# In a slot of the attention loop, the second step of a head's output in front of the first transposes of the next head

## The chip, the cores and the metric

The kernel runs on one NeuronCore of a Trainium2 chip. The metric is the device time of one execution in microseconds (us), lower is better. The core has five engines that work side by side, each through its own queue of instructions in a fixed order: TensorE (PE, matmuls; its weight loads are listed apart as PEld), VectorE (DVE), ScalarE (ACT), GpSimd (POOL) and SyncE (SP, which here only starts transfers, DMAs). An instruction starts when all before it in its queue have started and the semaphores that it waits for have been raised by other engines or by DMAs.

## The reference

Eight batches of eight heads of attention (576 positions, 64 dimensions a head) with a mask by blocks of 64, then a feed-forward part with a product of two projections:

```python
scores = scale * np.matmul(q, k.transpose(0, 1, 3, 2))     # q, k, v: (8, 8, 576, 64)
mask = (pos[:, None] // 64) >= (pos[None, :] // 64)
scores = np.where(mask, scores, -1000000000.0)
scores = scores - np.max(scores, axis=-1, keepdims=True)
attn = np.exp(scores)
attn = attn / (np.sum(attn, axis=-1, keepdims=True) + 1e-09)
attn_out = np.matmul(attn, v)
...
x = attn_out.transpose(0, 2, 1, 3).reshape(4608, 512)
out = ((x @ w_a) * (x @ w_b)) @ w_out                      # w_a, w_b: 512x1536, w_out: 1536x512
```

## The kernel before

The program has two parts. The first, up to about 640 us, is a loop over 66 slots (`for s in range(NH + LAG)`): it computes the attention of 64 heads and, between the attention's steps, the first pass of the feed-forward part (a third of the hidden columns) for the tokens that are done, 36 matmuls a slot in the long run. The second part, from there to the end, computes the other two thirds of the hidden columns, with weights that DVE unpacks from 64-bit numbers as it goes.

Three Python generators make a head's attention, and each call of `next` on one writes out a step of it:

- `softmax` (S): the head's scores in four blocks of query rows, each block's maximum (DVE, L398) and exponentials (ACT, L401). The last step sums up and inverts the sums (DVE, `rc`, L435 to L442), and POOL multiplies the five tiles of exponentials `e` by them (L445), first the tile of the last block, `e_3`.
- `turn` (T): four groups of transposes of the scaled `e` tiles by PE (L468, tiles `tp`), from block 3 down to block 0. I call them T3, T2, T1, T0. For each, ACT copies the result to `ah` (L470) and, from the ninth head on, DVE computes the remainder `al` (L472). The remainders of T1 and T0 are put behind the inversion `rc` of the next head in DVE's queue (`behind_of(..., "rc")`).
- `values` (V): the head's output. From the ninth head on its first step, V1, is four matmuls with `ah` (L517), and its second, V2, six matmuls that also read `al` (L521, L523), two copies by ACT (L527, L530) and four additions by DVE (L528 to L532). At every second head V2 also splits the finished x into two parts (ACT and POOL, L110 and L113: `xh`, `xl`) and starts a DMA of x to memory from ACT's queue (L539). For the first eight heads ("native", plain 32-bit matmuls) the output is one run of 16 matmul calls with `ah` alone (L499 to L512), split between the two steps.

A slot `s` runs the steps that the list `SLOT` names: which generator, for which head relative to `s`, and a weight `m` by which feed-forward matmuls are dealt out after the step. So a head's scores come in slot `s`, its T3, T2 and T1 in slot `s+1`, its T0, V1 and V2 in slot `s+2`. The loop counts the steps with a weight in `k`; at certain values of `k` it also writes out the split of the next pair's q and k (`split_q`, `split_k`: ACT L337 and L344, DVE L338, POOL L345) and the copying of these to both halves of the partitions (`spread`, DMAs).

The order in which Python writes the instructions out is not yet the order in the queues. A scheduler takes them by that order as a priority, but lets an engine go on with a later one where, by its own reckoning of time, an earlier one is not ready. A changed `SLOT` therefore moves instructions on all engines.

Buffers that matter here: the `tp` tiles in PSUM have two buffers, which T0 to T3 and the small output tile `av0` of V2 share in turn; the output tile `av` has one.

In front of the loop and in slots 0 and 1 some matmuls on zeros are put in (`WARM`, `KEEP`), whose results nobody reads. The weights of the first pass are unpacked in the first dozen slots by DVE (`convert`, L139 to L149, five instructions for each of twelve tiles), with one ACT instruction (L140) and copies by ACT and POOL.

Of the kernel before, what the change touches and what calls it, by code (L numbers as in the profile page):

```python
# [52 lines left out]
def attention_then_bilinear_ffn(  # L53
# [529 lines left out]
    def want(now):  # L583

        n = (now - H - LAG) * per_slot - behind
        if now < 2 * H + LAG:
# [6 lines left out]
    S_, T_, V_ = softmax, turn, values  # L593

    SLOT = [(S_, 0, 3), (S_, -1, 0), (T_, -2, 4), (S_, 0, 4), (V_, -2, 3), (S_, 0, 3),
            (T_, -1, 4), (V_, -2, 3), (S_, 0, 3), (T_, -1, 5), (T_, -1, 4)]
    fill = sum(m for _, _, m in SLOT)
    gens = {}
    for s in range(NH + LAG):
# [294 lines left out]
```

## Time and profile before

| what | value |
|---|---|
| median of three runs | 1281.07 us (1278.56 to 1282.27) |
| the profiled execution | 1281.83 us, its span 1279.8 us |
| busy share of the span | PE 97%, PEld 92%, DVE 78%, ACT 53%, POOL 43% |
| TensorE clock granted over the span | 0.988 of full speed |
| instructions | 23524, of them 7849 matmuls |

The span goes from the first to the last instruction; 2.0 us of the execution's time lie outside it. A busy share counts the time in which at least one of an engine's instructions is under way. The ends of matmuls are modelled and matmuls overlap, so a busy PE need not run at its peak. The granted clock is told as a share of full speed; 1.00 is 2.4 GHz and 0.50 is 1.2 GHz, and it knows only these two levels here.

### The profile page before, as it was taken

Reading aid. Unit: us, or ns where it says so; the run is one execution under the profiler, and the core shown is the slowest. Engines: PE = TensorE matmul, PEld = TensorE weight load, DVE = VectorE, ACT = ScalarE, POOL = GpSimd, SP = SyncE. Lnnn points to the kernel's source line nnn. Section 1 sums busy time; section 2 is a strip of 40 time slices with the busy share of each in tenths; the row PEclk is TensorE's granted clock in tenths of the full one; section 3 lists DMA queues with packets and bytes.
Section 4 is the critical chain, followed back from the end, with each engine's and each line's share of the span. In section 5 each row is a group of like instructions: output and inputs, shape, how many; then the busy total and the mean of one; then the engine's idle time right before and its main releaser. Section 6 shows DMA issues by size and latency. Waiting matters only on the chain.

```text
span 1279.8 us, 23524 instructions
## 1 busy us (share of the span) xinstructions
PE 1239.3 (97%) x7849; PEld 1173.2 (92%) x7849; DVE 999.2 (78%) x2389; ACT 683.6 (53%) x1722; POOL 554.9 (43%) x679
## 2 busy tenths in 40 slices
PE   9988999999999999999988998999999999999998
PEld 5668998999999999999988998999999999999998
DVE  6878887777887877877699999899967577577553
ACT  5788787788787788888745423233222222122210
POOL 4567565566665565665422322223223123123231
PEclk8999999999999999999998999999999999999999
DMA  5467766777767767676225355364466442243131
GB/s 195 132 167 201 187 174 175 178 171 181 170 167 179 179 171 176 167 178 155 87 94 171 100 180 194 139 206 164 141 220 244 145 149 79 70 149 98 52 99 62
DMA packets 93496, 196.58 MB, mean 154 GB/s; under 512 B 11968, under 2 KB 52928, under 8 KB 93376
## 3 DMA queue, kind: packets, MB, share of 16 engines
q1 hardware_dynamic: 88768, 185.64, 51.4%
q10 hardware_dynamic: 4608, 9.44, 2.0%
q8 instruction: 63, 1.03, 0.3%
q14 instruction: 57, 0.47, 0.1%
HBM read 96.47 MB, written 47.19 MB: 112 GB/s over the span
## 4 chain that ended last, share of the span: by engine, by line
PE 71%; DVE 15%; DMA 4%; issue 4%; ACT 3%; POOL 2%; SPq 1%; ACTq 0%; DVEq 0%; POOLq 0%
PE pso_z L754 13%; PE ps L217 12%; PE tp L468 7%; PE psx_z L708 6%; PE psw_z L708 6%; PE psv_z L708 6%; PE pso L217 4%; PE s L392 4%; PE psy_z L708 3%; PE av L517 3%; PE av L523 3%; PE sl L392 2%; DMA kp<-kT 2%; PE av L507 2%; DVE sw L147 1%
## 5 line engine op out<-in xcount | busy, mean ns | idle before, releaser
L113 POOL TENSOR_TENSOR h_z<-u_z,h_z 128x384 fp32r<-128x384 f32 x96 | 112.8, 1175 | 391.4 <-ACT h_z L110 379.8
L217 PE MATMUL ps<-xh,wab 128*128 128x288 f32 x1024 | 241.8, 304 | 1.2 <-ACT a L241 1.2
L754 PE MATMUL pso_z<-h_z,wo 128*128 128x384 f32 x1152 | 204.0, 335 | 4.5 <-POOL h_z L113 4.5
L445 POOL TENSOR_SCALAR e<-e,rc 128x512 f32<-128x512 f32 (+3 forms) x256 | 151.6, 604 | 127.9 <-DVE rc L442 118.1
L754 PEld LDWEIGHTS pso_z<-h_z,wo 128*128 128x128 f32 x1152 | 199.6, 188 | 7.0 <-POOL h_z L113 7.0
L217 PEld LDWEIGHTS ps<-xh,wab 128*128 128x128 f32 x1024 | 172.3, 189 | 4.7 <-ACT a L241 1.4
L472 DVE TENSOR_TENSOR al<-tp,ah 128x512 fp32r<-128x512 f32 x224 | 131.6, 608 | 31.5 <-ACT ah L470 31.0
L217 PE MATMUL ps<-xl,wab 128*128 128x288 f32 x512 | 154.1, 301 | 0.0
L468 PE MATMUL tp<-ident,e 128*128 128x128 f32 x832 | 136.1, 278 | 10.4 <-POOL e L445 4.0
L470 ACT CAST ah<-tp 128x512 fp32r<-128x512 f32 x224 | 116.4, 531 | 50.3 <-PE tp L468 47.5
L110 ACT CAST h_z<-u_z 128x384 fp32r<-128x384 f32 x96 | 49.3, 514 | 167.7 <-DVE u_z L733 160.2
L217 PE MATMUL pso<-hh,wo 128*128 128x288 f32 x512 | 128.1, 311 | 4.3 <-ACT hh L110 4.3
L708 PE MATMUL psx_z<-xh,wab 128*128 128x384 f32 x384 | 118.5, 344 | 7.2 <-DVE u_z L726 6.7
L468 PEld LDWEIGHTS tp<-ident,e 128*128 128x128 f32 x832 | 100.8, 142 | 25.7 <-POOL e L445 9.5
L401 ACT ACTIVATE e<-s,nm 128x192 f32<-128x192 f32 (+2 forms) x192 | 101.5, 529 | 32.4 <-DVE nm L398 23.2
L708 PE MATMUL psw_z<-xh,wab 128*128 128x384 f32 x384 | 117.0, 340 | 0.8 <-DVE u_z L728 0.8
L708 PE MATMUL psv_z<-xh,wab 128*128 128x384 f32 x384 | 116.7, 339 | 0.5 <-DVE u_z L730 0.4
L398 DVE TENSOR_REDUCE nm<-s 128x1 f32<-128x192 f32 (+3 forms) x256 | 109.9, 431 | 2.4
L217 PEld LDWEIGHTS ps<-xl,wab 128*128 128x128 f32 x512 | 96.5, 188 | 3.4
L217 PEld LDWEIGHTS pso<-hh,wo 128*128 128x128 f32 x512 | 88.3, 192 | 6.6 <-ACT hh L110 5.3
L113 POOL TENSOR_TENSOR v<-vr,v 128x320 fp32r<-128x320 f32 x56 | 50.2, 897 | 89.3 <-ACT v L110 67.9
L392 PE MATMUL s<-k,q 128*128 128x256 f32 x336 | 81.2, 322 | 2.2 <-ACT e_s L401 1.9
(142 smaller groups left out, 2919.5 us busy)
## 6 DMA issues: line engine op xcount, KB each, us to landing
k<-kp SPq DMA_DIRECT2D x112, 288.0 KB, 3.8
xr<-xd SPq DMA_DIRECT2D x48, 384.0 KB, 3.5
pt<-part SPq DMA_DIRECT2D x96, 192.0 KB, 3.5
q<-qp SPq DMA_DIRECT2D x112, 160.0 KB, 2.6
raww<-wab SPq DMA_DIRECT2D x24, 512.0 KB, 3.8
qp<-qT SPq DMA_DIRECT2D x32, 320.0 KB, 3.2
vr<-vm SPq DMA_DIRECT2D x64, 160.0 KB, 3.1
kp<-kT SPq DMA_DIRECT2D x32, 288.0 KB, 3.5
```

Source lines behind the costliest of these rows:

```text
L110: nc.scalar.copy(hi, src)
L113: return lo_eng.tensor_tensor(lo, src, f32(hi), op=ALU.subtract)
L217: mm = nc.tensor.matmul(ps, w_, d_, start=(i == 0), stop=(i == n - 1))
L392: mark = nc.tensor.matmul(ps[:, :w], qm[:, q0[t]:q0[t] + P], kk[:, :w], start=(i == 0), stop=(i == len(ks) - 1))
L398: nc.vector.tensor_reduce(nm[:, t:t + 1], view, axis=AX.X, op=ALU.max, negate=True)
L401: nc.scalar.activation(out, view, AF.Exp, bias=bias, accum_out=sm[:, t, :1])
L445: nc.gpsimd.tensor_scalar(ev, ev, rc[:, t:t + 1], 1.0, op0=ALU.mult, op1=ALU.mult)
L468: mark = nc.tensor.transpose(tp[:, c], src, ident)
L470: nc.scalar.copy(ah[:, :m, cols], tp[:, :m])
L472: return nc.vector.tensor_tensor(al[:, :m, cols], tp[:, :m], f32(ah[:, :m, cols]), op=ALU.subtract)
L708: nc.tensor.matmul(ps, wt[:, i, iw], j[:, ix], start=start and kp == 0 and i == 0 and j is xh, stop=kp == KP - 1 and i == 1, skip_group_ch ...
L754: nc.tensor.matmul(ps, wt[:, a, osl], b, start=i == 0, stop=i == 3 * len(fs) - 1)
```

## The change

Two neighbouring entries of `SLOT` change places. V2 of head `s-2` now comes before T3 of head `s-1`:

```diff
     SLOT = [(S_, 0, 3), (S_, -1, 0), (T_, -2, 4), (S_, 0, 4), (V_, -2, 3), (S_, 0, 3),
-            (T_, -1, 4), (V_, -2, 3), (S_, 0, 3), (T_, -1, 5), (T_, -1, 4)]
+            (V_, -2, 3), (T_, -1, 4), (S_, 0, 3), (T_, -1, 5), (T_, -1, 4)]
```

Every instruction of the program stays; the number of each kind is the same. The weights move with their steps: 3 units of feed-forward work now follow V2 at this place and 4 follow T3, where 4 and then 3 stood before. `spread` of an even slot is written out after the same number of steps, so now behind T3. Slots 0 and 1 have no V steps and stay as they were.

In a later slot, head 26 (`3_2`) having its V2 and head 27 (`3_3`) its T3, PE's queue reads as follows before (`ps` is feed-forward work, `av` the output, `tp` the transposes):

```order
L468 MATMUL tp3_3_3_4059<-ident_102,e1_3_120 128x128 x4
L217 MATMUL ps1_2_0_1_4042<-xh2_1_0_2970,wab1_81 128x288
L217 MATMUL ps1_2_0_1_4042<-xh2_2_0_3288,wab1_81 128x288
L217 MATMUL ps1_2_0_1_4042<-xl2_2_0_3289,wab1_81 128x288
L217 MATMUL ps1_2_0_1_4042<-xh2_2_0_3288,wab1_81 128x288
L521 MATMUL av03_2_4070<-ah3_2_3898,v23_2_3855 128x128
L521 MATMUL av03_2_4070<-al3_2_3899,v23_2_3855 128x128
L523 MATMUL av3_2_4034<-al3_2_3899,v23_2_3855 128x256
L523 MATMUL av3_2_4034<-al3_2_3899,v23_2_3855 128x320
L523 MATMUL av3_2_4034<-al3_2_3899,v23_2_3855 128x448
L523 MATMUL av3_2_4034<-al3_2_3899,v23_2_3855 128x512
```

and after:

```order
L521 MATMUL av03_2_4057<-ah3_2_3924,v23_2_3855 128x128
L521 MATMUL av03_2_4057<-al3_2_3925,v23_2_3855 128x128
L523 MATMUL av3_2_4034<-al3_2_3925,v23_2_3855 128x256
L523 MATMUL av3_2_4034<-al3_2_3925,v23_2_3855 128x320
L523 MATMUL av3_2_4034<-al3_2_3925,v23_2_3855 128x448
L523 MATMUL av3_2_4034<-al3_2_3925,v23_2_3855 128x512
L217 MATMUL ps1_2_0_1_4042<-xh2_1_0_2958,wab1_81 128x288
L217 MATMUL ps1_2_0_1_4042<-xh2_2_0_3276,wab1_81 128x288
L217 MATMUL ps1_2_0_1_4042<-xl2_2_0_3277,wab1_81 128x288
L468 MATMUL tp3_3_3_4076<-ident_102,e1_3_120 128x128 x4
```

V2 stands where T3 stood, and T3 behind V2 and three feed-forward matmuls; what precedes and follows is the same.

In slot 2, the first with all steps (`sl`, `s1` and the like are scores, `av0_0` the output of head 0, `tp0_1_3` T3 of head 1), the difference on PE is:

```order
 L507 MATMUL av0_0_341<-ah0_0_259,vr0_0_155 64x64
-L507 MATMUL av0_0_341<-ah0_0_259,vr0_0_155 64x128 x5
-L468 MATMUL tp0_1_3_357<-ident_102,e1_3_120 128x128 x4
+L507 MATMUL av0_0_341<-ah0_0_259,vr0_0_155 64x128 x7
 L392 MATMUL s10_2_307<-kp0_2_147,qp0_2_146 128x320
-L507 MATMUL av0_0_341<-ah0_0_259,vr0_0_155 64x128 x4
+L507 MATMUL av0_0_341<-ah0_0_259,vr0_0_155 64x128 x2
 L507 MATMUL av0_0_341<-ah0_0_259,vr0_0_155 64x64 x4
 L512 MATMUL av0_0_341<-ah0_0_259,vr0_0_155 64x64
+L468 MATMUL tp0_1_3_367<-ident_102,e1_3_120 128x128 x4
 L468 MATMUL tp0_1_2_386<-ident_102,e1_2_119 128x128 x4
```

T3 no longer cuts the output run and now stands directly in front of T2, so that eight transposes follow each other. From the first output matmul (L499) to T2 of head 8, PE changes 71 times between scores, transposes and output before, and 61 times after.

DVE's queue moves too. Before, the unpacking of the last weight tile of the first pass (`raww3_2`) stands between the remainder of T2 of head 9 (`al1_1`) and the maxima of head 11 (`nm1_3`):

```order
L472 TENSOR_TENSOR al1_1_1239<-tp1_1_2_1284,ah1_1_1238 128x4x128
L143 TENSOR_SCALAR mw3_2_1303<-raww3_2_1155 128x512
L147 SCALAR_TENSOR_TENSOR sw3_2_1302<-raww3_2_1155,sw3_2_1302 128x512
L145 SCALAR_TENSOR_TENSOR mw3_2_1303<-raww3_2_1155,mw3_2_1303 128x512
L413 MEMSET s11_3_1322 64x64
L149 TENSOR_TENSOR xw3_2_1304<-mw3_2_1303,sw3_2_1302 128x512
L414 MEMSET s11_3_1322 64x64
L398 TENSOR_REDUCE nm1_3_1318<-sl1_3_1321 128x1
```

After, the same place reads:

```order
L472 TENSOR_TENSOR al1_1_1255<-tp1_1_2_1284,ah1_1_1254 128x4x128
L413 MEMSET s11_3_1322 64x64
L243 TENSOR_TENSOR hf_0_0_0_1335<-ps1_0_0_0_1273,a_0_0_0_1271 128x288
L414 MEMSET s11_3_1322 64x64
L398 TENSOR_REDUCE nm1_3_1318<-sl1_3_1321 128x1
```

The five instructions of that tile now stand about two heads earlier, around the inversion `rc1_0` of head 8. On ACT and POOL the split of the next pair's k (L344, L345) moves in every second slot of the later part from the middle of the slot to its end, directly in front of the scaling of `e_3` on POOL. In the second part of the program, after the loop, the queues read the same.

## Rows read from the trace of the kernel before

**Rows 1.** The page, part 1: busy us (share of the span), instructions.

```profile
PE 1239.3 (97%) x7849; PEld 1173.2 (92%) x7849; DVE 999.2 (78%) x2389; ACT 683.6 (53%) x1722; POOL 554.9 (43%) x679
```

**Rows 2.** Stretches: us, busy of PE, PEld, DVE, ACT, POOL; clock; DMA share, GB/s.

```profile
27.00:30.50 3.50, 3.50 (x12) 2.00 (x10) 0.26 (x1) 1.96 (x6) 1.18 (x4) 0.50 0.46 152
30.50:34.10 3.60, 3.60 (x22) 3.46 (x22) 2.44 (x7) 1.41 (x6) 1.22 (x1) 0.50 0.00 0
34.10:41.00 6.90, 6.90 (x46) 4.42 (x44) 5.89 (x17) 5.73 (x17) 4.70 (x6) 1.00 0.33 101
...
76.00:100.00 24.00, 19.84 (x157) 16.29 (x155) 17.96 (x49) 19.66 (x52) 15.84 (x20) 1.00 0.63 171
100.00:130.00 30.00, 26.85 (x185) 24.17 (x184) 26.98 (x79) 24.05 (x67) 21.14 (x27) 1.00 0.68 188
...
201.40:204.80 3.40, 3.17 (x13) 3.13 (x14) 1.05 (x4) 1.47 (x4) 2.04 (x5) 0.50 0.95 196
204.80:640.00 435.20, 433.05 (x3122) 415.47 (x3122) 339.59 (x1075) 345.28 (x965) 259.33 (x373) 1.00 0.66 166
```

**Rows 3.** Timeline of PE, 38 to 43 us: start, us, instruction, count, [idle before <-releaser].

```profile
38.66 0.66 PE L468 MATMUL tp<-ident,e 128*128 128x128 f32 x4
39.25 1.09 PE L507 MATMUL av<-ah,vr 128*64 128x128 f32 x8
...
41.72 0.98 PE L468 MATMUL tp<-ident,e 128*128 128x128 f32 x7
...
42.75 0.48 PE L412 MATMUL s<-kp,qp 64*128 64x128 f32 x2
```

**Rows 4.** Timeline of PE, two of its waits between 108 and 113 us.

```profile
108.75 0.41 PE L468 MATMUL tp<-ident,e 128*128 128x128 f32 x2 [0.93 <-DVE al L472]
...
112.44 0.40 PE L217 MATMUL ps<-xh,wab 128*128 128x288 f32 x1 [1.17 <-ACT a L241]
```

**Rows 5.** Timelines of DVE and ACT, 108 to 112 us.

```profile
108.53 0.41 DVE L143 TENSOR_SCALAR mw<-raww 128x512 int32<-128x512 int32 x1
...
110.24 1.19 DVE L149 TENSOR_TENSOR xw<-mw,sw 128x512 f32<-128x512 f32 x1
...
111.47 0.62 ACT L110 CAST wo<-xw 128x512 fp32r<-128x512 f32 x1 [1.90 <-DVE xw L149]
```

**Rows 6.** Timelines of DVE, POOL and PE in one slot, 122 to 124 us.

```profile
122.70 0.98 DVE L472 TENSOR_TENSOR al<-tp,ah 128x512 fp32r<-128x512 f32 x2
...
122.88 1.30 POOL L445 TENSOR_SCALAR e<-e,rc 128x512 f32<-128x512 f32 x2 [0.89 <-DVE rc L442]
...
123.63 0.66 PE L468 MATMUL tp<-ident,e 128*128 128x128 f32 x4 [0.16 <-POOL e L445]
```

**Rows 7.** Timelines of ACT, POOL, DVE and PE, 198 to 203 us.

```profile
198.17 0.67 ACT L344 CAST kp<-kp 128x576 fp32r<-128x576 f32 x1 [0.84 <-DMA part<-ob]
...
198.92 1.42 POOL L345 TENSOR_TENSOR kp<-kp 128x576 f32<-128x576 f32 x1 [3.18 <-ACT kp L344]
200.30 1.88 POOL L445 TENSOR_SCALAR e<-e,rc 128x512 f32<-128x512 f32 x2
...
198.36 0.98 DVE L472 TENSOR_TENSOR al<-tp,ah 128x512 fp32r<-128x512 f32 x2
...
201.63 1.11 PE L468 MATMUL tp<-ident,e 128*128 128x128 f32 x4 [1.42 <-POOL e L445]
```

**Rows 8.** Timelines of POOL, DVE and PE in one slot, 299 to 303 us.

```profile
300.14 1.30 POOL L445 TENSOR_SCALAR e<-e,rc 128x512 f32<-128x512 f32 x2 [0.29 <-DVE rc L442]
...
299.96 0.98 DVE L472 TENSOR_TENSOR al<-tp,ah 128x512 fp32r<-128x512 f32 x2
...
301.08 0.60 PE L468 MATMUL tp<-ident,e 128*128 128x128 f32 x4
...
302.06 0.22 PE L521 MATMUL av<-ah,v 128*128 128x128 f32 x1
...
302.98 0.29 PE L217 MATMUL ps<-xh,wab 128*128 128x288 f32 x1
```

## The prediction

> **What bounds the kernel now.** I read four views in this order. The page says that PE has work under way for 97% of the span, DVE for 78% [rows 1]. The table of stretches says where PE is not busy: from 204.8 to 640 us it lacks 2.2 of 435.2 us, but from 76 to 100 us 4.2 and from 100 to 130 us 3.2 [rows 2]. It also shows the granted clock: 0.50, that is 1.2 GHz, in the stretch before 34.1 us and from 201.4 to 204.8 us. The timeline of PE then names the waits, and those of DVE, POOL and ACT say what each wait hung on [rows 4 to 8]. So the reader should see a PE-bound program, whose loop still holds some waits in the first 205 us and next to none later. A change of order can save no more than those waits, the cost of switching between kinds of matmul, and stretches at half clock; it can lose by making new ones.
>
> **The later slots: nothing.** T3 waits for the scaling of `e_3` on POOL, V2 for the remainder `al` of T0 on DVE, and both hang on the same inversion. At 299 to 303 us the two remainders behind it end at 299.96 + 0.98 = 300.94, and T3 starts at 301.08 [rows 8]. V2, put in this place, has 0.14 us to spare, some 0.06 more because its first matmul reads `ah` alone. T3 moves later by V2 (302.06 to 302.98 = 0.92) and three feed-forward matmuls (302.06 - 301.08 is T3 with four of them, 0.98; I put three at 0.40): 1.3 us, so POOL gets as much slack. Behind T3 stand T2 and T1, whose `tp` buffers come free after the additions of V2 and the remainder of T3. Those have about 3 us on PE before them, against some 2 us of copies and additions, and I cost that at nothing; without that cover it would be a few tenths a slot. The split of the next k, 0.67 on ACT and 1.42 on POOL [rows 7], now stands just before the scaling in every second slot. The 1.3 us by which T3 moves and the slack before it cover that; if k came late from memory they would not (rival B). The DMAs move with their steps: that of x starts about 1 us earlier on ACT's queue and is read only in the second part; those of `spread`, SP's queue included, keep their place among the steps, two slots before their data are read. From 205 to 640 us I put 0, and for the part after the loop 0, where the order is the same.
>
> **The first slots: switches, -1.2 us.** In the plain 32-bit heads T3 cut the output run. What a cut costs: four transposes take from 38.66 to the next start at 39.25, 0.59 us; eight in one run 41.72 to 42.75, 1.03 us [rows 3]. Two runs of four would take 1.18, so a run more costs 0.15. The order shows ten changes of kind fewer, so at most 10 x 0.15 = -1.5. PE has no idle time to speak of between 51 and 76 us, so most of this counts. Some of it lies after 76 us, where PE waits anyhow; I take -1.2 (bounds 0 and -1.5).
>
> **Slots 10 to 12: the unpacking leaves, -2.0 us.** At 108.75 and 112.44 us PE waits 0.93 and 1.17 us, for a remainder on DVE and for a copy on ACT [rows 4]. DVE unpacks the last weight tile there: four instructions from 108.53 to 110.24 + 1.19 = 111.43, and ACT sits 1.90 us waiting for it with that copy behind it in its queue [rows 5]. In the new order these instructions stand about two heads earlier, and feed-forward work enters PE's queue earlier. The second wait should go, the first nearly so. Bounds: 0, if DVE is as late two heads earlier, and -2.1; I take -2.0, near the row.
>
> **At 201.6 us: -2.2 us.** Here k came late: ACT splits it at 198.17, POOL has it done at 200.3, only then scales `e_3`, and T3 starts at 201.63 after 1.42 us of idle PE. The remainders that V2 needs were there at 198.36 + 0.98 = 199.34 [rows 7]. With V2 and three feed-forward matmuls (1.3 us) in front, T3 finds `e_3` ready: -1.4. Right after the wait the clock was 0.50 for 3.4 us [rows 2]; work at half clock takes twice as long, so this stretch cost 1.7. I take half of it, -0.8 (bounds 0 and -1.7), since PE idles just before too.
>
> **New waits: +0.3 us.** Between 110 and 170 us T3 did wait for POOL, 0.16 us at 123.63 [rows 6]. But the remainders end at 122.70 + 0.98 = 123.68, so V2 in its place waits just as long and about 0.05 more. With six or seven such slots: +0.3 (0 to +1).
>
> The sum is -1.2 - 2.0 - 2.2 + 0.3 = -5.1 us. Against the profiled execution (span 1279.8, time 1281.83) that gives 1276.7; this execution was 0.8 slower than the median of 1281.07, from which the sum would give 1276.0. I forecast 1276.5. Its own range is 1273 to 1280.
>
> **Rival A: no change, 1281 us.** The waits of the first 205 us come back elsewhere. For it: the scheduler moved instructions in all queues, V2's condition and T3's end within 0.1 us of each other [rows 6], and a late k still holds POOL. Against it: the unpacking is gone from where it hurt, and the switches are saved whatever waits. With the switches alone the time is 1281.8 - 1.2 = 1280.6, with new waits 1281 to 1282.
>
> **Rival B: the clock rises later, 1285.5 us.** Before 34.1 us PE works without a gap at 1.2 GHz, scores and transposes among its work, and stays there in 27.0 to 30.5; the clock is 1.00 from 34.1 on, after a long output run [rows 2]. The new order makes the output run of slot 2 start and end earlier and puts eight transposes behind it, then scores. If that is not what raises the clock, it stays at 1.2 GHz through the scores and transposes up to the next long output run: the 6.9 us from 34.1 to 41.0 would take up to 6.9 more. That outweighs all my gains (-5.1) once it lasts for over 5.1 us of work; with one head more (3.4) it is +10.3. So 1276.7 + 6.9 = 1283.6 to 1287; the middle is 1285.5. Against it: the run itself is as long as before, and little else comes between. The Trainium skill (TensorE: Matmul & The Clock Gate, section Part 4: PE-mode transpose) says that transposes do not count as PE being busy in the same way for the full clock. The rows agree in so far as a busy share of 3.50 in 3.50 us did not raise it; that transposes are the reason no run here shows. By that rule this rival would come true.
>
> **Rival C: PE waits in every later slot.** If the remainder of T0 comes 0.4 us later than in rows 8, because ACT's copy for it now stands behind the split of k, V2 waits 0.2 us in each second slot of the last 46: 23 x 0.2 = +4.6, which cancels the gains, 1281.3. It adds to A.
>
> **How the numbers follow.** Forecast 0.46, A with C 0.32, B 0.22. The forecast's median lies beyond 0.3% (3.8 us, about what a measurement of this kernel can tell from no change; the border is 1277.2), part of its range does not, and a clock that needs no rescue at 201 us could add to it: faster 0.45. No change takes A, C and the slow edge of the forecast's range, less what of them drops out on either side: 0.34. Slower is B: 0.21. The range goes from below the forecast's own (both half-clock stretches that the rows show after 34 us gone, -1.7 more) to the middle of B: 1272 to 1286.
>
> **What would show it.** In the new profile: 8 transposes in a run after the output in slots 2 to 8; no wait of PE over 0.5 us at 105 to 115 us; no wait for POOL of over 1 us in T3 after 130 us; PE lacking about 2 us between 205 and 640 as before. The clock's first rise at 34 us or earlier speaks for the forecast, at 37 us or later for rival B. The forecast is wrong if waits `av <- DVE al` appear in PE's list by more than 2 us, or if the low clock lasts longer than before over the first 60 us.

## The result: slower by 0.5%, and the profile after

The changed kernel takes 1284.99 us in the median of eight runs (1284.02 to 1288.9); the kernel before, run beside it, 1279.8 (1275.98 to 1284.03). The ratio is 1.0047, with an interval of 1.0027 to 1.0068: 5 to 6 us slower, where I had forecast 4.6 faster. The profiled execution took 1284.32 us, 2.5 more than the one of before; its span is 1282.5. It lies near the low end of its runs and that of before above its median, so the two traces show less of a difference than the medians.

The page's first part and the table of stretches answer [rows 1, 2]; the columns are the same.

```profile
PE 1233.5 (96%) x7849; PEld 1169.8 (91%) x7849; DVE 996.8 (78%) x2389; ACT 686.4 (54%) x1722; POOL 560.1 (44%) x679
```

```profile
20.50:34.10 13.60, 12.85 (x83) 8.40 (x82) 12.96 (x37) 10.83 (x31) 10.68 (x12) 1.00 0.32 103
...
51.00:76.00 25.00, 23.86 (x154) 17.83 (x153) 19.90 (x54) 19.45 (x55) 16.44 (x19) 0.87 0.65 184
...
100.00:130.00 30.00, 27.34 (x182) 25.36 (x181) 22.52 (x71) 22.96 (x64) 18.38 (x25) 0.94 0.72 181
201.40:204.80 3.40, 3.40 (x28) 3.31 (x27) 2.70 (x9) 2.58 (x7) 1.37 (x2) 1.00 0.81 179
204.80:640.00 435.20, 425.72 (x3067) 407.02 (x3066) 336.49 (x1063) 343.31 (x954) 260.54 (x371) 1.00 0.64 164
```

PE lacks 435.20 - 425.72 = 9.48 us from 204.8 to 640 us, where it lacked 2.15 [rows 2]. The wait and the half clock at 201 us are gone. The half clock before 34 us is gone too, but there is some between 51 and 76 and between 100 and 130 us.

To see where the time goes I set the inversion `rc` of the same head beside itself in the two traces (after minus before):

| head | time before | difference | what lies between |
|---|---|---|---|
| 3 | 44.76 | -5.38 | half clock at 20 to 34 us, of the two in before alone |
| 8 | 93.55 | -2.45 | half clock at 51 to 58 us, after alone |
| 18 | 188.37 | -1.76 | |
| 20 | 211.41 | -5.30 | the wait of T3 for a late k and the half clock behind it |
| 21 | 221.32 | -3.82 | a late q, 1.18 us |
| 30 | 308.99 | -2.73 | |
| 40 | 406.82 | -2.36 | |
| 50 | 504.61 | -0.61 | |
| 63 | 628.56 | +2.04 | |

So at 211 us the sum of the prediction, -5.1, seems to hold, and the 43 later slots, which I had put at nothing, take 7.3 back. The list of PE's waits says on what:

```profile
PE tp L468 <- DVE al L472: 8.2, 31, 0.4
```

Transposes wait for a remainder `al` 31 times, 8.2 us in all (2.8 us in 7 times before). It is not T3, and not V2 either: no wait of V2 (L521) stands in the list. From 213 us on T1 waits so in about every fourth slot and T0 in about every second. In a slot with an odd head's V2, PE's timeline reads (T3, T2, T1, and T0 in the next slot):

```profile
289.13 0.60 PE L468 MATMUL tp<-ident,e 128*128 128x128 f32 x4
...
290.90 0.60 PE L468 MATMUL tp<-ident,e 128*128 128x128 f32 x4
...
292.51 0.52 PE L468 MATMUL tp<-ident,e 128*128 128x128 f32 x3 [0.35 <-DVE al L472]
...
295.42 0.41 PE L468 MATMUL tp<-ident,e 128*128 128x128 f32 x2 [0.26 <-DVE al L472]
```

ACT in the same stretch:

```profile
289.44 0.58 ACT L530 COPY avlo<-av 64x512 f32<-64x512 f32 x1
289.92 0.46 ACT L110 CAST v<-vr 128x320 fp32r<-128x320 f32 x1
290.29 0.74 ACT L337 ACTIVATE qp<-qp 128x640 fp32r<-128x640 f32 x1
291.05 0.59 ACT L470 CAST ah<-tp 128x512 fp32r<-128x512 f32 x1
...
291.53 0.77 ACT L110 CAST xh<-xf 128x288 fp32r<-128x288 f32 x2
292.93 0.63 ACT L401 ACTIVATE e<-s,nm 128x448 f32<-128x448 f32 x1 [0.63 <-DVE nm L398]
...
293.55 0.39 ACT L241 COPY a<-ps 128x288 f32<-128x288 f32 x1
293.83 1.09 ACT L470 CAST ah<-tp 128x512 fp32r<-128x512 f32 x2
```

And DVE:

```profile
291.67 0.69 DVE L472 TENSOR_TENSOR al<-tp,ah 128x512 fp32r<-128x512 f32 x1 [0.48 <-ACT ah L470]
292.28 0.61 DVE L398 TENSOR_REDUCE nm<-s 128x1 f32<-128x448 f32 x1
294.11 0.46 DVE L243 TENSOR_TENSOR hf<-ps,a 128x288 f32<-128x288 f32 x1 [1.22 <-ACT a L241]
294.58 0.11 DVE L413 MEMSET s<- 64x64 f32 x1
294.60 0.67 DVE L472 TENSOR_TENSOR al<-tp,ah 128x512 fp32r<-128x512 f32 x1
```

`tp` has two buffers that the steps take in turn: V2's small tile, T3, T2, T1, T0. So T1 takes T3's buffer and T0 takes T2's. T3 is done on PE by 289.7, but ACT copies it at 291.05 only, behind V2's copy, v and q; its remainder ends at 292.36, and T1 starts at 292.51. DVE's maximum `nm`, ACT's exponential behind it, `a` and only then the copy of T2 are late by the same amount, so the remainder of T2 ends at 295.27, and T0 starts at 295.42. Before, T1 took the buffer of V2's tile (order T3, V2, T2, T1), and ACT copied T3 while PE did V2, in front of q and v. The same slot before, ACT, DVE and PE (T3, the first matmul of V2, T2, T1):

```profile
291.89 0.58 ACT L470 CAST ah<-tp 128x512 fp32r<-128x512 f32 x1
...
293.19 0.74 ACT L337 ACTIVATE qp<-qp 128x640 fp32r<-128x640 f32 x1
...
292.51 0.69 DVE L472 TENSOR_TENSOR al<-tp,ah 128x512 fp32r<-128x512 f32 x1 [0.61 <-ACT ah L470]
...
291.20 0.60 PE L468 MATMUL tp<-ident,e 128*128 128x128 f32 x4
...
292.17 0.22 PE L521 MATMUL av<-ah,v 128*128 128x128 f32 x1
...
294.31 0.60 PE L468 MATMUL tp<-ident,e 128*128 128x128 f32 x4
...
295.41 0.49 PE L468 MATMUL tp<-ident,e 128*128 128x128 f32 x3
```

T3's remainder was done at 293.20, 1.1 us before T2 took its buffer.

The event at 201 us [rows 7] went as forecast. POOL still splits k in front of the scaling, but PE has work until then (POOL's and PE's timelines; the latter are V2 and T3):

```profile
195.37 1.44 POOL L345 TENSOR_TENSOR kp<-kp 128x576 f32<-128x576 f32 x1 [1.84 <-ACT kp L344]
196.93 1.31 POOL L445 TENSOR_SCALAR e<-e,rc 128x512 f32<-128x512 f32 x2
```

```profile
197.81 0.22 PE L521 MATMUL av<-ah,v 128*128 128x128 f32 x1
...
199.14 0.60 PE L468 MATMUL tp<-ident,e 128*128 128x128 f32 x4
```

In slot 10, where the waits of [rows 4] are gone, a new one stands, and it shows the same queue. ACT waits 1.94 us in front of the split of k, whose transfer had started at 96.71 us and took 4.8. V2's copy `avlo` is queued behind it, so V2's small tile stays taken, and T2, which now takes that buffer, waits (PE, then ACT):

```profile
103.54 0.63 PE L468 MATMUL tp<-ident,e 128*128 128x128 f32 x4 [1.79 <-ACT avlo L530]
```

```profile
101.54 0.67 ACT L344 CAST kp<-kp 128x576 fp32r<-128x576 f32 x1 [1.94 <-issue]
...
102.75 0.26 ACT L527 COPY avlo<-av 64x128 f32<-64x128 f32 x1
```

### The profile page after: what moved, and what is told of

The parts are those of the page before. It is cut to its first block, busy times and chain, and to the rows that moved or that the text cites. A ratio compares the mean times of both kernels' runs of the same rounds, so it can differ in the third digit from the quotient of the medians.

```text
span 1282.5 us, 23499 instructions
## 1 busy us (share of the span) xinstructions
PE 1233.5 (96%) x7849; PEld 1169.8 (91%) x7849; DVE 996.8 (78%) x2389; ACT 686.4 (54%) x1722; POOL 560.1 (44%) x679
## 4 chain that ended last, share of the span: by engine, by line
PE 51%; DVE 12%; ACT 3%; issue 3%; DMA 1%; POOL 1%; SPq 0%; ACTq 0%; DVEq 0%; POOLq 0%
PE pso_z L754 14%; PE psw_z L708 6%; PE psx_z L708 6%; PE psv_z L708 6%; PE ps L217 5%; PE pso L217 3%; PE psy_z L708 3%; PE tp L468 3%; PE s L392 2%; PE av L517 1%; PE av L523 1%; DVE al L472 1%; DVE sw L147 1%; DVE mw L145 1%; DVE mw L172 1%
## 5 line engine op out<-in xcount | busy, mean ns | idle before, releaser
L445 POOL TENSOR_SCALAR e<-e,rc 128x512 f32<-128x512 f32 (+3 forms) x256 | 157.4, 628 | 116.0 <-DVE rc L442 108.5
L401 ACT ACTIVATE e<-s,nm 128x192 f32<-128x192 f32 (+2 forms) x192 | 101.6, 529 | 36.1 <-DVE nm L398 26.3
L398 DVE TENSOR_REDUCE nm<-s 128x1 f32<-128x128 f32 (+3 forms) x256 | 109.5, 430 | 2.3
L113 POOL TENSOR_TENSOR hl<-hf,hh 128x288 fp32r<-128x288 f32 x64 | 53.9, 842 | 74.7 <-ACT hh L110 74.7
L708 PEld LDWEIGHTS psx_z<-xh,wab 128*128 128x128 f32 x384 | 71.5, 189 | 12.5 <-DVE u_z L726 12.5
```

Of the source, the lines that this page charges most:

```text
L113: return lo_eng.tensor_tensor(lo, src, f32(hi), op=ALU.subtract)
L398: nc.vector.tensor_reduce(nm[:, t:t + 1], view, axis=AX.X, op=ALU.max, negate=True)
L401: nc.scalar.activation(out, view, AF.Exp, bias=bias, accum_out=sm[:, t, :1])
L445: nc.gpsimd.tensor_scalar(ev, ev, rc[:, t:t + 1], 1.0, op0=ALU.mult, op1=ALU.mult)
L708: nc.tensor.matmul(ps, wt[:, i, iw], j[:, ix], start=start and kp == 0 and i == 0 and j is xh, stop=kp == KP - 1 and i == 1, skip_group_ch ...
```

## The experiments

The first column of the table is the edit; "PE lacks" is 435.2 us less PE's busy time from 204.8 to 640 us in the profiled execution; the ratio is to the kernel before on the same chip, with its 95% interval; "half clock" is the mean over the runs of the time at 1.2 GHz, worked out from each run's recorded mean clock as 2 x (1 - clock) x time, with its standard error.

| V2 in front of T3 | ratio | PE lacks | half clock, us (runs) |
|---|---|---|---|
| nowhere (before) | 1 | 2.2 | 26.3 ± 0.8 (75) |
| everywhere (the change) | 1.0047 (1.0027 to 1.0068) | 9.5 | 25.7 ± 1.6 (8) |
| slots 0 to 20 | 1.001 (0.9996 to 1.0024) | 5.4; again 3.0 | 31.2 ± 1.8 (12) |
| slots from 21 | 1.0045 (1.0027 to 1.0062) | 8.5 | 23.2 ± 2.0 (12) |
| slots 0 to 9 | 1.0012 (0.9996 to 1.0027) | 2.7 | 33.7 ± 1.7 (12) |
| slot 20 | 0.999 (0.9977 to 1.0004) | 3.3 | 24.7 ± 0.9 (12) |
| even slots from 20 | 1.0006 (0.9987 to 1.0024) | 2.0 | 29.6 ± 0.9 (12) |
| odd slots from 21 | 1.0084 (1.0056 to 1.0111) | 8.5 | 27.9 ± 2.5 (6) |

**Early or late slots.** In all these kernels the step list is chosen by slot; `SLOT` is that of before.

```diff
+    SWAPPED = [*SLOT[:6], (V_, -2, 3), (T_, -1, 4), *SLOT[8:]]
...
-        for what, i, m in SLOT:
+        for what, i, m in (SWAPPED if s < 21 else SLOT):
```

> V2 stands before T3 in slots 0 to 20 only; from slot 21 on the order of before. Theory (the later slots lose: in every second slot T1 waits about 0.33 us and T0 about 0.2 us for the remainder al whose tp buffer they take, some 7.4 us more idle PE from 205 to 640 us): PE lacks about 2 us from 205 to 640 us as before, the end comes 7 us earlier than with the change everywhere, ratio to before about 0.998 (0.996 to 1.000). Rival (the loss is made in the first 205 us, by the clock or by waits, and only shows in the median): ratio about 1.004, as with the whole change.

With `s >= 21` instead:

> V2 stands before T3 from slot 21 on only; slots 0 to 20 in the order of before. Theory (the later slots lose): PE lacks about 9 us from 205 to 640 us, ratio to before 1.006 (7.4 us). Rival (the loss is made early): PE lacks 2 to 4 us there and the ratio is within 1.000 to 1.002.

The late slots alone give the whole loss, 1.0045 against 1.0047, with PE lacking 8.5 us. The early slots alone give neither the gain I expected nor the rival's loss. PE lacked 5.4 us later on, most of it in four waits at scores, 2.9 us, and in the waits for a remainder behind them; at the first, at 273 us, ACT had waited 2.03 us for k from memory. The same program once more:

> The same program as the one with the swap in slots 0 to 20 only, once more. If the waits at scores behind a late k at 273, 391, 412 and 472 us (PE lacking 5.4 us from 205 to 640 us) belong to the order, they come at the same places and of about the same length; if they hang on when the transfers happen to land, PE lacks between 2 and 5 us, at other places. Half clock in the first 100 us, 13.7 us there, is expected to lie elsewhere and to have another length.

It lacked 3.0 us, at other places (317, 358, 417, 534, 554 us, 0.3 to 0.8 us each), so place and length of these waits are not set by the order; that they hang on when transfers land fits this, but two executions do not show it. Half clock lay at 55 to 62 and 76 to 83 us, against 51 to 58 and 71 to 78.

With `s < 10`:

> V2 stands before T3 in slots 0 to 9 only, the heads in plain 32-bit. Theory: fewer switches and another clock in the first 60 us bring head 8 some 2 to 3 us earlier; the event at 201 us (T3 waits 1.4 us for POOL, then half clock for 3.4 us) stays as before; ratio about 0.999. Rival (the whole early gain lies in slots 10 to 20): ratio 1.000 and head 8 at the time of before, within 0.5 us.

Head 8 came 1.66 us later than in before's trace, not 2 to 3 earlier. Between the inversions of heads 9 and 10 it gained 2.45 us, where the waits of [rows 4] are gone (one of 0.89 us came in their place), and it kept 2.2 of this to head 19; the wait at 201 us stood as before. In time nothing is left, which fits the 33.7 us that these runs spend at half clock.

**Which slots, later.** With `s >= 20 and s % 2 == 0`, and with `s >= 21 and s % 2 == 1`:

> The kernel before, with V2 in front of T3 in the even slots from 20 on alone; ACT's queue in the odd slots, which hold the split of q and of x, is that of before. Theory (T1, and T0 of the next slot, wait only where ACT and DVE have the splits of q and x between V2 and T3's remainder, in the odd slots): PE lacks 1 to 3 us from 205 to 640 us, the wait at 201 us is gone, ratio 0.998. Rival (V2 in front makes T1 or T0 wait for its buffer in any slot): PE lacks 5 us there, half of what the change loses, ratio 1.001.

> The kernel before, with V2 in front of T3 in the odd slots from 21 on alone. Theory (the odd slots make the whole loss): PE lacks 8 to 9 us from 205 to 640 us, ratio 1.006, as with the swap in all slots from 21 on. Rival (even and odd slots share the loss): PE lacks 5 us, ratio 1.003.

The stretch from 204.8 to 640 us, first with the even slots, then with the odd ones:

```profile
204.80:640.00 435.20, 433.24 (x3126) 415.68 (x3124) 344.32 (x1073) 343.06 (x961) 261.43 (x374) 1.00 0.66 165
```

```profile
204.80:640.00 435.20, 426.67 (x3066) 406.55 (x3065) 333.88 (x1066) 344.85 (x955) 259.15 (x372) 1.00 0.65 165
```

This decides where it is lost: the odd slots make the whole of the idle time, the even ones none. The two kinds differ in what ACT has behind V2's copies: in the odd slots v and the split of q in front of T3's copy and the split of x behind it; in the even ones v stands behind T3's copy and there is no split of q or x. An even slot with the even slots swapped (ACT, T3's copy and v; PE, T1 without a wait):

```profile
298.21 0.57 ACT L470 CAST ah<-tp 128x512 fp32r<-128x512 f32 x1
298.67 0.47 ACT L110 CAST v<-vr 128x320 fp32r<-128x320 f32 x1
...
300.15 0.49 PE L468 MATMUL tp<-ident,e 128*128 128x128 f32 x3
```

In time the odd slots cost more than the whole change, 1.0084 against 1.0047, with intervals that overlap. From the inversion of head 20 to that of head 63 the two profiles lose the same, 7.4 us against before; the rest of the odd slots' loss lies elsewhere, in the profiled execution behind the loop (4.9 us more than before), and is not explained.

**What in the odd slots.** Three ways to bring T3's copy forward on ACT. First q's and k's split behind T3:

```diff
+            if k == 7 and odd and s + 1 < NH and s >= 21:
+                split_q((s + 1) // 2)
+                split_k((s + 1) // 2)
+                spread(s + 1)
+                spread(s + 2)
```

(with the two old places limited to `s < 20`).

> The whole change, and from slot 20 on the split of the next pair's q and k (with their spread) is written out behind T3 of the odd slot instead of in the even slot before it; in ACT's queue the copy of T3 then stands in front of the copy of v and of the 0.74 us instruction on q; the matmuls from V2 to T1 keep their order on PE. Theory (T1 waits because ACT copies T3 late, behind v and q): the waits of T1 go, PE lacks under 4 us from 205 to 640 us, ratio about 0.999. Rival (T3 stands too near to T2 and T1 on PE, whatever ACT does): T1 still waits about 0.3 us in every second slot, 7 us, ratio about 1.004. Second rival (a late q or k now holds the scores): new waits of PE at scores (L392) of over 2 us.

Ratio 1.0126 (1.0106 to 1.0147), PE lacks 18 us. T1's waits did go, but for three of 1.0 us in all. But T0 waits about 0.5 us in every second slot, and scores wait 6.8 us, for q's instruction now stands on ACT in front of the next head's first exponentials. PE's waits from 205 to 640 us:

```profile
PE tp L468 <- DVE s L413: 8.5, 17, 0.6
PE s L392 <- ACT e_s L401: 4.7, 6, 1.3
PE s L412 <- DMA q<-qp: 2.1, 1, 2.1
```

The first line is T0: the memset `s` that it names stands right behind T2's remainder in DVE's queue. So the theory is right on T1, the second rival came true as well, and the time is lost. Then v's split alone:

```diff
-            if k == 1 and 0 < s <= NH:
+            if k == (5 if s > 20 else 1) and 0 < s <= NH:
```

> The whole change; from slot 21 on the split of v (ACT 0.46 us, then POOL) is written out behind V2 instead of behind T0, which in the odd slots puts ACT's copy of v behind the copies of T3 to T0, while the instruction on q (0.74 us) stays in front of the copy of T3. PE keeps its order from V2 to T1. Theory (T1 waits for ACT's queue): ACT copies T3 about 0.4 us earlier, and the waits of T1 (0.33 us every fourth slot, 0.06 every other) go; T0's waits shrink too; PE lacks 3 to 5 us from 205 to 640 us instead of 9.5; ratio about 1.002. Rival (T3 too near to T1, whatever ACT does): T1 waits as in the changed kernel, PE lacks 9 us, ratio 1.005. Second rival (v in front of the exponentials of the next head delays these): new waits at scores.

Ratio 1.0085 (1.0061 to 1.0109). The same slot as above, T1 and T0 on PE:

```profile
293.72 0.52 PE L468 MATMUL tp<-ident,e 128*128 128x128 f32 x3
...
296.46 0.41 PE L468 MATMUL tp<-ident,e 128*128 128x128 f32 x2 [0.49 <-DVE s L413]
```

T1 no longer waits there (it does in four other slots, 2.0 us in all), and PE came to T0 sooner by as much: T0 waits 0.49 where it waited 0.26, as T2's copy still stands on ACT behind the exponential and `a`. PE lacks 11.1 us, not 3 to 5. Last, T3 straight behind V2:

```diff
-            (V_, -2, 3), (T_, -1, 4), (S_, 0, 3), (T_, -1, 5), (T_, -1, 4)]
+            (V_, -2, 0), (T_, -1, 7), (S_, 0, 3), (T_, -1, 5), (T_, -1, 4)]
```

> V2 in front of T3 everywhere, but with no feed-forward matmuls between them: the three that stood there follow T3 (weights 0 and 7 instead of 3 and 4). ACT's copy of T3 then stands in front of v and q in the odd slots. T3 comes 0.40 us earlier, T2 and T1 at the same time as in the changed kernel. Theory: T1's waits go, PE lacks 2 to 4 us from 205 to 640 us, ratio 0.999 to 1.001. Rival (the tp buffers are the wall in any order with V2 in front): PE lacks 9 us, ratio 1.005. Second rival (T3 now waits for POOL's scaling): waits of T3 on POOL of over 2 us in all.

T1's waits went but for one and T0's stayed (0.19 to 0.26 us in nearly every second slot); PE lacks 7.0 us, 1.5 of it in the one wait of T1, at 219.6 us, where ACT had waited 1.02 us for q. The ratio is 1.0041 (1.002 to 1.0061), about what 4.8 us more of idle PE make. All three show the same: T1 waits for ACT's queue and not for PE's distance to T3, which the first two kernels left alone. T0's wait, the other half of the loss, stayed in all three: the rows put it down to the chain that runs on over `nm`, the exponential and T2's copy, and this is read, not shown by an edit. Whether moving the split of x would be enough for it was not tried.

**The terms of the first slots by themselves.** With `s == 20`:

> The kernel before, with V2 in front of T3 in slot 20 alone, where T3 waits 1.42 us for POOL behind a late k and 3.4 us at half clock follow. Theory (the term of 2.2 us at 201 us was real): that wait goes and the half clock there with it, all else as before, 3 us less, ratio 0.998. Rival (the gain is given back by later waits for k, as in the kernel with the swap in slots 0 to 20): ratio 1.000, and PE lacks 5 us from 205 to 640 us.

From head 18 to head 20 the difference to before goes from -2.53 to -5.73: 3.2 us, as forecast by the theory, of which 2.3 are left at head 63 (-4.81). The ratio is 0.999, with 1 inside its interval; the medians are 1276.6 and 1278.65. With `CONV0 = 2` in addition:

> The kernel before with the swap in slot 20 alone, and with the unpacking of the first pass's weights written out one tile earlier (CONV0 2 instead of 1), which puts the last tile where the changed kernel has it, about two heads earlier. Theory (the term of 2.0 us for slots 10 to 12 was real and is independent of the swap): no waits of 0.9 and 1.2 us of PE between 105 and 113 us, 2 us less than with slot 20 alone, ratio 0.997. Rival (DVE is then late for the heads before, and the same waits come earlier): PE idle from 60 to 105 us grows by 2 us, ratio 0.999.

Both waits between 105 and 113 us went, and from the inversion of head 9 to that of head 10 it gained 3.5 us; a wait of 1.61 us at 125.7 us took 1.8 of this back. And PE is idle for 6.5 us in the first 60 us, where it was for 4.2 with slot 20 alone (one wait of 2.58 us at 18 us among them): the rival was right in kind, further ahead than I had looked: from 60 to 105 us PE is idle 3.7 us against 4.5. With it come 36.9 ± 1.5 us at half clock against 24.7. The ratio is 1.0008 (0.9988 to 1.0028).

So no kernel of these clearly beats the one before; the swap in slot 20 alone comes nearest.

## Why the prediction was wrong

- **The later slots, "Behind T3 stand T2 and T1 ... I cost that at nothing": this step failed.** I had the right place (the `tp` buffers) and the right price without cover ("a few tenths a slot"), but took the cover from PE's 3 us against 2 us of copies and additions. In the odd slots ACT has V2's two copies, v and q (0.46 + 0.74) in front of T3's copy: the remainder ends 292.36 - 289.13 = 3.2 us after T3's start, and T2's 295.27 - 290.90 = 4.4 us after T2's. Measured: T1 waits 0.35 and T0 0.26 there, 9.5 us of idle PE instead of 2.2 from 205 to 640 us, and the difference is all in the odd slots. I had counted durations and not the queue in which they stand; the order of ACT around L337 was there to be read.
- **Rival C** had the size of this (+4.6) and the wrong place: V2 never waited for T0's remainder, so the place of this loss was in none of my cases. "New waits, +0.3" for V2 were not there either.
- **At 201.6 us, -2.2:** right mechanism, under-sized. Wait and half clock went wholly: -3.2 with slot 20 alone, -3.5 in the change. The half that I kept of the half clock had no ground.
- **Slots 10 to 12, -2.0:** the unpacking does leave, and its two waits go (2.45 us with the swap in slots 0 to 9). In the changed kernel T2 waits 1.79 and T1 0.40 us in the same slot for buffers behind a late k on ACT, the failed step once more (in four of the five other executions with the swap in slot 10, T2 waits 0.74 to 1.70 us and T1 0.41 to 0.51): the difference to before is -2.45 at head 8 and -2.40 at head 12.
- **The native switches, -1.2: no gain in time.** From the inversion of head 2 to that of head 9, the kernel before and four executions of its order there, and three of the new order (the experiments on T3's copy), have 3.4 us at half clock each. The old order takes 65.40 to 65.62 us, the new one 65.64 to 66.18; the changed kernel, with 6.8 us at half clock, 66.41. PE is idle 5.4 to 5.9 us in the old and 7.3 to 7.4 in the new. So it is busy for 0.6 to 1.9 us less, which fits the switches but does not show them, and new waits take as much, which the term had left out. One stands in all seven executions of the new order, T1 waiting for POOL's scaling (here the changed kernel):

```profile
49.12 0.52 PE L468 MATMUL tp<-ident,e 128*128 128x128 f32 x3 [1.25 <-POOL e L445]
```

- **Rival B** had the wrong place. In the changed kernel's trace the clock did not fall at 20 us at all. In four other executions of the new order it fell at 18.0 to 20.4 us and was back at 28.3 to 34.1, no later than with the old order (27.6 to 34.1). The rule of the Trainium skill (TensorE: Matmul & The Clock Gate, section Part 4: PE-mode transpose) that I weighed there did not decide. In one of the four the clock rose at 34.1 us, as eight transposes in a row ended (T3 in front of T2 in slot 2, in the kernel with T3 straight behind V2):

```profile
32.40 1.88 PE L468 MATMUL tp<-ident,e 128*128 128x128 f32 x8
```

But half clock does come later in the swapped native slots: from 53.2 to 83 us, behind the stretch at 44 to 53 us that the old order has, the granted clock was 1.00 in all six executions with the old order there, and 0.77 to 0.94 in all seven with the new. Over the whole run the changed kernel has no more of it than before (25.7 us against 26.3). One place is slot 8, where in three of the seven (not in the changed kernel) the output waits 1.50 to 2.11 us for a copy `ah` that is queued on ACT behind a q late from memory; here PE's wait, ACT's queue and the stretch behind it with the swap in slots 0 to 20:

```profile
71.64 0.47 PE L499 MATMUL av<-ah,vr 128*64 128x64 f32 x2 [1.50 <-ACT ah L470]
```

```profile
70.38 0.74 ACT L337 ACTIVATE qp<-qp 128x640 fp32r<-128x640 f32 x1 [0.74 <-DMA qp<-qT]
71.02 0.57 ACT L470 COPY ah<-tp 128x512 f32<-128x512 f32 x1
```

```profile
71.40:78.30 6.90, 6.66 (x32) 5.68 (x33) 5.61 (x12) 4.05 (x14) 4.24 (x4) 0.51 0.53 112
```

- **What of the -5.30 at 211 us was the order's?** Less than it looks: the -3.5 at 201 us. The rest, -1.8, was there before, left of -2.45 at head 8. The swap from slot 21 on has the old order in the first slots, and its trace stood at -4.71 at head 8, with 14 us less at half clock up to there. So the clock of single executions, without any change of order, makes differences as large as this one, and I compared with an execution that had 17 us at half clock between 20 us and head 8.

The early slots alone came out at 1.001, +1.3 us. An estimate of its parts: -3.2 is slot 20, where 3.4 us at half clock went too; these runs have 4.9 us more of it than before all the same, so 8.3 more elsewhere, +2.5 (at 0.30 us each, below); about +1.5 is the new wait of slot 8, while slots 10 to 12 give and take the same. That is +0.8; the other 0.5 us are not accounted for, and the interval (-0.5 to +3.1 us) is wider than that.

## What to carry to other kernels

Before a producer of a rotating buffer is moved, list for every later user of that buffer which instruction now frees it, and read what stands in front of that instruction in its engine's queue, above all instructions that wait for memory. Durations alone say that there is cover; the queue says whether it is used. A difference between two single profiles in a stretch with different clocks is no gain until the same order has been seen twice.

## What was not expected of the hardware

Half clock goes along with about half of what differs between runs of one program (by its variance): over 75 runs of the kernel before, with 1272 to 1287 us, 0.30 us of time go with each us at half clock (correlation 0.70). By the two clock levels alone it would be 0.5 if PE bound the kernel throughout. Stretches at half clock began within 2 us of the end of a wait of PE at 47.8 and 201.4 us before and at 105.3 us after, at waits of 1.27, 1.42 and 1.79 us, so that such a wait can cost more than it lasts: 3.2 us for the 1.42. Others of that length, as that of 1.34 us at 81.7 us after, had none behind them.
